# Attention and a snake MLP in one kernel: another order for the first two stages

## The chip, the cores and the metric

The kernel runs on one core of one Trainium2 chip. The metric is the device time of one execution in microseconds (us); it is the median of several runs. All times below are in microseconds unless marked otherwise. Five engines work side by side, each through its own queue in order: TensorE (PE, with its weight loads PEld), VectorE (DVE), ScalarE (ACT), GpSimd (POOL) and SyncE (SP). DMAs are issued by SP, ACT and POOL; all of them run on the same 16 DMA engines.

## The reference

Eight batches, twelve heads, 448 positions, head width 64. The queries and keys are normalised by their root mean square, attention follows, and its output (3584 tokens, 768 wide) goes through an MLP with a snake activation:

```python
q_n, k_n = rmsnorm(q, g_q), rmsnorm(k, g_k)
scores = q_n @ k_n.T / sqrt(64)
attn = softmax(scores)              # over the keys
x = (attn @ v), heads side by side  # 3584 x 768
h = x @ w_in                        # 768 x 2048
g = h + sin(alpha * h)**2 / (alpha + 1e-9)
out = g @ w_out                     # 2048 x 768
```

Inputs and output are f32; the matmuls run in bf16.

## The kernel before, in words

The work goes batch by batch, one stage per batch. A stage computes the attention of batch b, then h and g of batch b (`first_product`, L460), while the product with w_out of batch b-1 (`second_product`, L498) is cut into small filler steps that stand between the pieces of attention. Stage 0 has no fillers. After the last stage the last product runs by itself.

The twelve heads of a batch are three chunks of four (chunk index ci, three per batch, so ci 0 to 2 belong to batch 0). For each chunk: load q and k (`load_qk`, L155, on SP's queue, the k of chunk 0 on ACT's), square them (`square`, L274: on ACT for ci 0 and 1, on POOL after that), fold g_q times g_k into q (`fold_g`, POOL, L283), sum the squares (`reduce`, DVE, L288), take the inverse root (`rsqrt`, ACT, L292; for ci up to 3 the result lies in PSUM and holds a pair of banks), scale to bf16 (`scale`, L302: DVE for ci up to 3, POOL after that), and transpose, for ci 0 to 2 with PE (`pe_transpose`, L323, whose copies out of PSUM are on DVE or ACT), later with DMA transposes on SP's queue (L315). The tiles of q and k have three buffers, so chunk ci + 3 is loaded when chunk ci has been scaled.

Per batch there are 21 score tiles (3 chunks of 7): four matmuls into a pair of PSUM banks and one exp on ACT (`scores`, L348). Five running products use the exp tiles (`attend`, L385): sums and values of chunk 0 ("ones 0", "values 0") and of chunks 1 and 2 ("ones 1", "low 1", "high 1"). A finished sum becomes a reciprocal by Ln and Exp on ACT (L431, L432), a finished value product is multiplied by it on DVE into xT (L440). h then runs over xT with all of w_in: 16 blocks m, two per PSUM pair; Sin on ACT (L446), its square on POOL for even m and on ACT for odd m (L449, L451), the sum on DVE (L454).

PSUM is four pairs of banks. Which pair each user gets is written out by hand as a string of digits per stage, taken one by one (`bank_pair`, L134); a user waits until the last user of that pair is through.

The order is also written out by hand, as a string of tokens per stage (`STAGE_0`, `STAGE_1`, and `STAGE_N` for the rest), and each engine's queue holds its part of the tokens in that order. A token is a letter and its arguments: `q` square, `u` reduce, `g` fold_g, `r` rsqrt, `k` scale, `p` transpose with PE, `t` transpose with DMA, each with the chunk's number counted from the stage's first chunk, then which (0 is q, 1 is k) and, if need be, which heads; `l` loads q and k of a chunk. `S` is the next score tile, and `Sn` puts n dummy matmuls of 512 columns ahead of it; `bn` is n dummies alone. `o`, `v`, `x`, `y`, `z` go on with "ones 0", "values 0", "ones 1", "low 1", "high 1" by so many tiles j. `F` (or a number n, which is n times F) is the next filler step of the oldest unit, `f` one of the unit after it; a unit has 8 steps of 8 matmuls, and step s needs blocks 2s and 2s + 1 of w_out. `G` spreads the gains, `L` spreads alpha (one small matmul and a copy each). `W` and `O` load a piece of w_in (`W` half, third) and a quarter of w_out (`O` hi, lo: rows of blocks 8 hi + 4 lo and the next three), `V` a part of v of a later or the same batch (0, 1 or 2: one, three or two of the six head pairs), all on POOL's queue with a cast to bf16. `D` lets POOL wait for a chunk's k, so that what POOL issues behind it starts later. The third member of a stage lists tokens that stand beside h: key -1 early in it, key i after blocks 2i and 2i + 1, key 8 at its end.

## Time and profile before

| | |
|---|---|
| three runs | 407.88, 408.73, 409.87; median 408.73 |
| profiled execution: span of its instructions | 405.8 |
| profiled execution: its own time outside the span | not given |
| busy in the span | PE 391.4 (96%), DVE 240.6 (59%), ACT 315.3 (78%), POOL 283.6 (70%) |
| h of batch 0, first to last matmul group | 35.60 to 54.49 |
| h of batch 1 begins | 81.50 |

A row of a timeline gives the start, the duration of all its instructions together, the engine, the line, the operation with its tiles and shapes, the count, and in brackets how long the engine had been idle before and what ended that. A row of the chain gives start, duration and what held up the end. A busy PE is not PE at its peak, since the ends of matmuls are modelled.

### The profile page before, as it was taken

The page shows a single profiled execution, that of the slowest core. Times are in us where ns is not written, and L with a number is a line of the kernel's source. Part 1 is how long each engine was busy: PE and PEld are TensorE (multiplying, and loading weights), DVE is VectorE, ACT ScalarE, POOL GpSimd, SP SyncE. Part 2 cuts the span into 40 slices and gives each one's busy share as a digit, 9 for nine tenths or more (in the row PEclk, how much of TensorE's full clock was granted, in tenths as well). Part 3 has the DMA queues.
Part 4 walks back from the last instruction along what each step waited for, and adds up shares of the span by engine and source line. Part 5 has one row for each costly group of instructions (what it writes and reads, how often), then busy time and mean ns, then how long its engine had stood idle before and what let it go on. Part 6 is the DMA issues. An engine that isn't in the chain of part 4 may idle for free.

```text
span 405.8 us, 15218 instructions
## 1 busy us (share of the span) xinstructions
PE 391.4 (96%) x6755; PEld 238.8 (59%) x6758; DVE 240.6 (59%) x364; ACT 315.3 (78%) x474; POOL 283.6 (70%) x268
## 2 busy tenths in 40 slices
PE   1999999999999999999999999999999999999996
PEld 1346467645675566755676556755667556765564
DVE  4956665756783576638584475836685485544512
ACT  5798889868896879958898678958898679877600
POOL 5998889987959789588877779597895784003300
PEclk9999999999999999999999999999999999999999
DMA  7999999855286925697076923879046901620022
GB/s 266 215 254 241 210 221 255 193 155 171 53 164 162 151 94 88 182 198 153 3 140 178 200 102 70 185 158 209 3 94 179 166 2 22 108 61 1 2 78 79
DMA packets 67846, 55.46 MB, mean 137 GB/s; under 512 B 41524, under 2 KB 63172, under 8 KB 67780
## 3 DMA queue, kind: packets, MB, share of 16 engines
q1 hardware_dynamic: 56578, 41.43, 42.2%
q0 software_dynamic: 10432, 11.81, 19.0%
q8 instruction: 53, 0.87, 0.9%
q10 hardware_dynamic: 770, 1.25, 0.9%
q14 instruction: 13, 0.11, 0.1%
HBM read 45.62 MB, written 11.01 MB: 140 GB/s over the span
## 4 chain that ended last, share of the span: by engine, by line
PE 88%; POOL 5%; DMA 3%; issue 1%; DVE 1%; ACT 1%; SPq 0%; POOLq 0%
PE hps L468 34%; PE ops L548 31%; PE av L416 9%; PE sc L357 7%; PE ops L529 5%; POOL sq L281 2%; DMA qk<-in_q_dram 2%; DMA qk<-in_k_dram 2%; PE av L404 1%; POOL qk L286 1%; POOL w_out_sb L248 1%; POOL w_in L241 1%; ACT expT L360 1%; DVE g_sb L454 0%; DVE xT L440 0%
## 5 line engine op out<-in xcount | busy, mean ns | idle before, releaser
L360 ACT ACTIVATE expT<-sc 128x896 bf16<-128x896 f32 x168 | 143.7, 917 | 7.4 <-PE sc L357 6.6
L548 PE MATMUL ops<-w_out_sb,g_sb 64*64 64x384 bf16 x3072 | 148.0, 323 | 0.0
L468 PE MATMUL hps<-xT,w_in 128*128 128x448 bf16 x768 | 147.0, 353 | 0.4 <-DVE g_sb L454 0.4
L468 PEld LDWEIGHTS <-w_in 128*128 128x128 bf16 x768 | 74.4, 98 | 72.5 <-issue 3.9
L454 DVE SCALAR_TENSOR_TENSOR g_sb<-s,inv_alpha_sb,hps 128x448 bf16<-128x448 f32 x128 | 81.1, 676 | 59.1 <-POOL s L449 58.5
L548 PEld LDWEIGHTS <-g_sb 64*64 64x64 bf16 x3072 | 91.9, 107 | 37.0 <-issue 3.8
L449 POOL TENSOR_TENSOR s<-s 128x448 f32<-128x448 f32 x64 | 59.6, 932 | 65.7 <-ACT s L446 43.9
L446 ACT ACTIVATE s<-hps,alpha_sb 128x448 f32<-128x448 f32 x128 | 73.9, 627 | 37.7 <-PE hps L468 37.2
L309 POOL TENSOR_TENSOR qkn<-qk,inv 128x448 bf16<-128x448 f32 x80 | 72.9, 938 | 24.6 <-issue 17.1
L281 POOL TENSOR_TENSOR sq<-qk 128x896 f32<-128x896 f32 x44 | 73.3, 1678 | 3.9 <-DVE ms L290 3.0
L357 PE MATMUL sc<-qkT 64*64 64x448 bf16 x672 | 60.3, 357 | 0.7 <-ACT expT L360 0.3
L286 POOL TENSOR_TENSOR qk<-qk,gg 128x896 f32<-128x896 f32 (+1 forms) x25 | 50.5, 2021 | 2.2 <-ACT g_sb L278 1.5
L554 DVE COPY osb<-ops 128x384 f32<-128x384 f32 x48 | 26.7, 556 | 38.5 <-PE ops L548 38.3
L290 DVE TENSOR_REDUCE ms<-sq 128x14 f32<-128x896 f32 x44 | 46.4, 1078 | 3.3 <-POOL sq L281 3.2
L440 DVE TENSOR_TENSOR xT<-av,rec 128x896 bf16<-128x896 f32 (+1 forms) x26 | 25.7, 1016 | 26.8 <-ACT rec L432 21.4
L451 ACT ACTIVATE s<-s 128x448 f32<-128x448 f32 x64 | 36.9, 577 | 2.9 <-DVE g_sb L454 0.7
L416 PE MATMUL av<-expT,vb 64*32 64x448 bf16 (+1 forms) x1120 | 38.1, 350 | 0.0
L357 PEld LDWEIGHTS <-qkT 64*64 64x64 bf16 x672 | 21.7, 107 | 13.8 <-issue 6.7
L555 DVE TENSOR_TENSOR osb<-osb,ops 128x384 f32<-128x384 f32 x48 | 26.6, 554 | 1.7
L416 PEld LDWEIGHTS <-vb 64*32 64x32 bf16 (+1 forms) x1120 | 20.8, 96 | 11.0 <-issue 2.2
L429 DVE TENSOR_REDUCE rec<-rec 32x448 f32<-32x448 f32 x28 | 17.1, 610 | 9.7 <-ACT rec L425 9.4
L529 PE MATMUL ops<-w_out_sb,g_sb 128*128 128x384 bf16 (+1 forms) x144 | 21.0, 309 | 0.0
(51 smaller groups left out, 185.8 us busy)
## 6 DMA issues: line engine op xcount, KB each, us to landing
qk<-in_q_dram SPq DMA_DIRECT2D x23, 448.0 KB, 5.2
qk<-in_k_dram SPq DMA_DIRECT2D x23, 448.0 KB, 5.7
out_dram<-osb SPq DMA_DIRECT2D x45, 192.0 KB, 2.9
w_out_sb<-in_moe_w_out_dram POOLq DMA_DIRECT2D x4, 768.0 KB, 12.8
w_in<-in_moe_w_in_dram POOLq DMA_DIRECT2D x6, 512.0 KB, 12.2
vb<-in_v_dram POOLq DMA_DIRECT2D x16, 168.0 KB, 7.2
vb<-in_v_dram POOLq DMA_DIRECT2D x8, 224.0 KB, 5.3
out_dram<-osb SPq DMA_DIRECT2D x13, 96.0 KB, 4.3
```

What stands on the lines that cost most here:

```text
L281: nc.gpsimd.tensor_mul(st.sq[w], qk[ci][:, w], qk[ci][:, w])
L286: nc.gpsimd.tensor_mul(x, x, gg.to_broadcast([P, len(heads) * NJ, D]))
L290: nc.vector.reduce_sum(st.ms[:, w, rows], st.sq[w][:, rows], axis=AX.X)
L309: eng.tensor_mul(n[:, :, hi, :], x[:, hi], inv[:, hi].unsqueeze(2).to_broadcast([P, NJ, D]))
L357: nc.tensor.matmul(sc[o:o + 64, hi, :S], qkt[r, 1, j * REST:(j + 1) * REST], qkt[r, 0, :], start=True, stop=True)
L360: nc.scalar.activation(expT[c, j], sc[:, :, :S], ACT.Exp, scale=SCALE)
L416: nc.tensor.matmul(av[o, k, :S], w, x[r, hi, :], start=(j == 0), stop=(j == last))
L446: nc.scalar.activation(s1, hps, ACT.Sin, scale=alpha_sb[:, m, :])
L449: nc.gpsimd.tensor_mul(s2, s1, s1)
L454: nc.vector.scalar_tensor_tensor(g_sb[:, m, (b % 2) * S:(b % 2 + 1) * S], s2, inv_alpha_sb[:, m, :], hps, op0=ALU.mult, op1=ALU.add)
L468: nc.tensor.matmul(ps[:, m % 2, :S], w_in_sb[m * 2 // MT][:, kt, m % (MT // 2) * P:(m % (MT // 2) + 1) * P], x[:, kt, :], start=(kt == ORD ...
L548: nc.tensor.matmul(st["ps"][os, r, :HALF], g_sb[rs, m, c0 + o * 64:c0 + o * 64 + 64], w_out_sb[rs, m, half * HALF:(half + 1) * HALF], star ...
```

## The change

The tokens of the first two stages are put in another order, with other strings of PSUM pairs. Dummy matmuls (`b`) stand from the start of stage 0's queue, before L and G. V00, V01 and a quarter of w_out (O10) come early, the three tokens D are gone, W11, W10 and W12 move to the beginning of h (key -1), O01 and O11 into h, and the loads of v for batch 1 from the end of h to stage 1. The products o, v, x, y, z are cut into shorter runs. Some helpers change to allow this: a square and the copies after a transpose can name their engine (`A`, `P`, `D`), and the PSUM pair of an rsqrt is given back when its own scalings are done, not when all four of the chunk are.

```diff
 STAGE_0 = (
     (
-        "q000 u000 q010 G q011 q001 u010 g00 u011 r01 g01 D1 u001 k01 r00 k00 q11 u11 O00 q10 V00 p012 "
-        "W01 q20 p00 g1 u10 r1 q21 u20 V01 g2 S4 V02 S k11 l3 k10 S1 S1 S4 W00 W02 S u21 r2 p1 L S2 S q31 "
-        "S3 k21 q30 k20 D2 S S3 o3 l4 g3 S W10 W12 o1 o3 p2 u30 l5 S3 u31 S1 S W11 S4 v7 S S S q40 S S x5 "
-        "y3 q41 u41 x1 g4 z4 u40 x1 r4 y4 O01 q50 z3 r3 O10 "
+        "b2 V00 q010A b3 b4 b3 q000A b2 u000 u010 q001A L b1 G V01 q011A u011 b4 r01 O10 u001 k01 r00 b5 q10A "
+        "g01 q11A b1 g00 b1 p01A k00 p00A u10 g1 u11 r1 q20P b2 q21P g2 b1 S1 S3 k10 S2 k11 S u20 S2 p1D u21 "
+        "S S1 b1 W01 l3 r2 V02 S2 k20 k21 S S1 S3 p2D q31P S o2 o2 S o1 S l4 u31 W00 v1 q41 v2 q30P u41 O00 "
+        "o2 S5 S2 q40 u30 W02 S v1 v3 S y1 z1 S z2 z1 u40 S y4 S x2 x5 y1 y1 z3 g3 "
     ),
-    "012311203203312021021302301231032103021321302",
-    {-1: 'u50 O11 k30', 0: 'D4 k401', 1: 'k411', 2: 'q51', 3: 'k31 k400 u51', 5: 'k410', 7: 'g5 V12', 8: 't3 V10 V11 t4 l6 l7'},
+    "2321230132031232210031031203310210321301321302121213032103",
+    {-1: 'W11 r3 r4 l5 k31 k30 q50 g4 u50 W10 t3 W12 q51 g5', 0: 'k410', 2: 'k400 O01 l6', 4: 'u51 O11 k411', 6: 'k401', 7: 'q60 t4'},
 )
 STAGE_1 = (
     (
-        "4 r2 f f k20 1 f f 2 k21 S 1 q31 1 t2 S 1 S 2 S q30 2 S 2 S S 3 f S 3 S 1 f S 1 S 1 u31 2 l5 g3 "
-        "S u30 o1 o6 1 r3 V10 2 S f q41 1 f 2 S 2 S 2 q40 S u41 1 v1 v1 S v3 V12 S k31 q50 v2 u40 S 2 S "
-        "V11 g5 S z4 x7 y7 r4 z3 g4 k30 "
+        "1 f S r2 f f f 1 f q31 2 S u30 f 1 S 1 k20 1 l4 2 f 1 u31 S V00 V01 1 k21 S 3 S q40 1 S 2 S o2 o5 S "
+        "2 r3 S 4 f V02 1 q41 t2 1 S 2 g4 k31 S 3 S 1 S 2 u41 S 2 v1 S v2 S v2 v2 S 2 S 1 S y4 x1 y1 x3 S 2 "
+        "x3 z2 u40 y2 z2 z3 "
     ),
-    "1320201203203013133213130101301231203123",
-    {-1: 'u50 t3', 0: 'k41', 2: 'k40', 5: 'q51', 6: 'l6 t4', 8: 'u51 l7'},
+    "2103030201201302101301321213213310231023",
+    {-1: 'g3 V10 k30 V11 r4 k40 l5 t3 k41 q50 l6', 0: 'l7 t4 q51', 1: 'V12', 3: 'u51', 5: 'g5 u50'},
 )
...
-        def square(w, heads=(0, 1)):
+        def square(w, heads=(0, 1), engine=None):
             if ci < 2:
                 st.sq[w] = spare(2 * ci + w).rearrange("p (a d) -> p a d", d=D)
-                rows = slice(heads[0] * NJ, (heads[-1] + 1) * NJ)
-                nc.scalar.activation(st.sq[w][:, rows], qk[ci][:, w, rows], ACT.Square)
+            elif w not in st.sq:
+                st.sq[w] = npool.tile([P, 2 * NJ, D], F32, tag="sq", name="sq")
+            rows = slice(heads[0] * NJ, (heads[-1] + 1) * NJ)
+            x, out = qk[ci][:, w, rows], st.sq[w][:, rows]
+            if (engine or ("A" if ci < 2 else "P")) == "A":
+                nc.scalar.activation(out, x, ACT.Square)
             else:
-                st.sq[w] = npool.tile([P, 2 * NJ, D], F32, tag="sq", name="sq")
-                nc.gpsimd.tensor_mul(st.sq[w], qk[ci][:, w], qk[ci][:, w])
+                nc.gpsimd.tensor_mul(out, x, x)
...
             inv = bank_pair("inv") if early else ln
-            if early:
-                st.inv_ps.append(inv)
+            held = SimpleNamespace(ps=inv, left=2 * len(range(2)[ws]))
             for w in range(2)[ws]:
-                st.inv[w] = inv[:, w, :2 * NJ]
+                st.inv[w], st.inv_ps[w] = inv[:, w, :2 * NJ], held
...
-            st.scaled += len(heads)
-            if st.scaled == 4:
-                for ps in st.inv_ps:
-                    give_back(ps)
+            held = st.inv_ps[w]
+            held.left -= len(heads)
+            if early and held.left == 0:
+                give_back(held.ps)
...
-        def pe_transpose(pairs, ws=(0, 1), act=0):
+        def pe_transpose(pairs, ws=(0, 1), engines="D"):
...
-                if act == 1 or act == 2 and pp == 0:
+                engine = engines[pp % len(engines)]
...
+                if engine == "A":
                     nc.scalar.copy(out, src)
                 else:
                     nc.vector.tensor_copy(out, src)
```

## Rows read from the trace of the kernel before

**Rows 1.** The page: the chain that ended last, shares of the span by engine.
```profile
PE 88%; POOL 5%; DMA 3%; issue 1%; DVE 1%; ACT 1%; SPq 0%; POOLq 0%
```

**Rows 2.** The chain in order of time: start, duration, what.
```profile
40.69 0.94 POOL s L449
41.66 1.28 DVE g_sb L454 x2
...
54.49 3.70 PE ops L548 x88
...
81.50 1.62 PE hps L468 x8
...
99.96 2.40 PE ops L548 x56
...
128.61 18.27 PE hps L468 x96
```

**Rows 3.** Timeline of ACT in stage 0.
```profile
10.75 0.51 ACT L339 COPY qkT<-tp 128x448 bf16<-128x448 bf16 x1
13.43 0.32 ACT L299 ACTIVATE inv<-ms,eps 128x28 f32<-128x28 f32 x1 [2.17 <-DVE ms L290]
...
13.92 3.32 ACT L360 ACTIVATE expT<-sc 128x896 bf16<-128x896 f32 x4
...
26.32 7.46 ACT L360 ACTIVATE expT<-sc 128x896 bf16<-128x896 f32 x9
```

**Rows 4.** Timeline of PE in stage 0.
```profile
11.22 1.89 PE L352 MATMUL sc<-blank 128*128 128x512 bf16 x4
...
26.71 1.04 PE L352 MATMUL sc<-blank 128*128 128x512 bf16 x4
...
35.60 4.71 PE L468 MATMUL hps<-xT,w_in 128*128 128x448 bf16 x24
```

**Rows 5.** Timeline of DVE in stage 0.
```profile
0.87 0.27 DVE L201 MEMSET blank<- 128x256 uint32 x1 [0.87 <-PEq L665]
...
7.09 1.15 DVE L290 TENSOR_REDUCE ms<-g_sb 128x7 f32<-128x448 f32 x2 [0.63 <-ACT g_sb L278]
8.30 2.21 DVE L309 TENSOR_TENSOR qkn<-qk,inv 128x448 bf16<-128x448 f32 x4
10.43 1.08 DVE L290 TENSOR_REDUCE ms<-g_sb 128x14 f32<-128x896 f32 x1
```

**Rows 6.** Windows: length, busy by engine, granted PE clock, DMA share, GB/s.
```profile
10.00:20.00 10.00, 9.44 (x94) 3.59 (x90) 9.12 (x17) 7.50 (x14) 9.97 (x10) 1.00 1.01 214
```

**Rows 7.** Timeline of POOL in stage 0.
```profile
6.07 1.13 POOL L286 TENSOR_TENSOR qk<-qk,gg 128x448 f32<-128x448 f32 x1 [1.14 <-ACT g_sb L278]
...
14.95 1.67 POOL L281 TENSOR_TENSOR sq<-qk 128x896 f32<-128x896 f32 x1
...
17.89 2.10 POOL L286 TENSOR_TENSOR qk<-qk,gg 128x896 f32<-128x896 f32 x1
...
27.65 2.18 POOL L241 DMA_DIRECT2D w_in<-in_moe_w_in_dram  x3
```

**Rows 8.** DMA queues, 8.5 to 9.0 (q1 SP's): packets, MB, share.
```profile
q1 hardware_dynamic: 119, 0.20, 105.2%
```

**Rows 9.** DMA queues, 16.5 to 17.0 (q0 is POOL's; V loads).
```profile
q0 software_dynamic: 54, 0.05, 57.8%
q1 hardware_dynamic: 52, 0.09, 56.4%
```

**Rows 10.** DMA issues, 2.3 to 3: KB each, median us to landing.
```profile
qk<-in_k_dram SPq DMA_DIRECT2D x1, 448.0 KB, 6.5
```

**Rows 11.** DMA queues, 12 to 14: all that moved.
```profile
q0 software_dynamic: 253, 0.39, 110.2%
```

**Rows 12.** DMA issues, 9 to 9.9.
```profile
w_out_sb<-in_moe_w_out_dram POOLq DMA_DIRECT2D x1, 768.0 KB, 7.7
```

**Rows 13.** DMA issues, 38 to 39.
```profile
w_out_sb<-in_moe_w_out_dram POOLq DMA_DIRECT2D x2, 768.0 KB, 15.0
```

More of the change, by code (lines that the diff above doesn't have):

```diff
@@ L266, in norm_tasks @@
         st.ms = npool.tile([P, 2, 2 * NJ], F32, tag="ms", name="ms")
-        st.inv, st.inv_ps, st.scaled = {}, [], 0
+        st.inv, st.inv_ps = {}, {}
         st.sq, st.n = {}, None
@@ L578, in step @@
     def step(b, token):
-        what, n = token[0], [int(x) for x in token[1:]]
+        what, n = token[0], [int(x) for x in token[1:] if x.isdigit()]
+        engines = [x for x in token[1:] if not x.isdigit()]
         if what == "b":
@@ L610, in step @@
             elif what == "q":
-                st.square(n[1], n[2:] or (0, 1))
+                st.square(n[1], n[2:] or (0, 1), *engines)
             elif what == "u":
@@ L620, in step @@
             elif what == "p":
-                st.pe_transpose((0, 1), n[1:2] or (0, 1), act=n[2] if n[2:] else 0)
+                st.pe_transpose((0, 1), n[1:2] or (0, 1), engines or "D")
             elif what == "t":
```

## The prediction

> **What bounds the kernel now.** I read the chain of waits first. PE's own work makes up 88% of it [rows 1]. The chain in order of time [rows 2] says where the rest is: until 40.69 it runs through POOL, its DMA issues and the q and k loads; then DVE frees a PSUM pair, and from there to the end it is PE. So after the h product of batch 0 the time is a sum of matmuls that the change does not alter: stage 1 has 48 filler steps and 21 score tiles before and after. What the change can move is when that h product ends (54.49 [rows 2]) and how densely stage 1 is packed. Stage 1 takes 27.0 from there to its own h (81.50); the stage after it takes 28.65 (99.96 to 128.61) with 8 filler steps more, each 0.336 (88 matmuls, 11 steps, in 3.70). At that density stage 1 would take 25.95, so about 1.05 is the most to be had there.
>
> The start is read from the timeline of ACT [rows 3]. The first exp begins at 13.92, after the inv of pair chunk 1 waited 2.17 for DVE's sums. The 21st exp ends at 26.32 + 7.46 = 33.78. Between them ACT has 21 exps of 0.83, a reciprocal and an inv, and nearly no gap: 19.9 that end with ACT, whatever PE does. The h product begins at 35.60 [rows 4], 1.82 later. So stage 0 is: first exp, plus 19.9, plus a tail of 1.82, plus 18.89 for h (35.60 to 54.49), where stage 1's h takes 18.46 (81.50 to 99.96).
>
> **The change, part by part.** The sum is made against the profiled execution: its span is 405.8, its own time outside the span isn't shown, and the runs (407.88 to 409.87, median 408.73) are 2.1 to 4.1 longer. I take it as the median run, 2.9 around the span.
>
> *Dummies ahead of G.* Fourteen dummy matmuls, then L, one more dummy and G now stand at the head of PE's queue, where G alone had been. PE is free once blank is zero, at 1.14 [rows 5]. A dummy took 0.47 at 11.22, just after PE had been idle, and 0.26 at 26.71 [rows 4], for 512 columns each: the 1.2 GHz level of the clock and the 2.4 GHz level. So the fourteen end between 4.8 and 7.7. I take 6.8, near the low level, since PE comes from idling here too. L, a dummy, G and the copy of gg add about 1.3, an estimate from those prices: gg at 8.1, with bounds 6.1 and 9.0. The granted clock, on the other hand, is given as 1.00, the 2.4 GHz level, from 10 to 20 [rows 6], over those 0.47 dummies. The Trainium skill (TensorE: Matmul & The Clock Gate, Seeing it yourself) warns that the trace's clock events have been unreliable; by the granted clock as written the fourteen would end at 4.8, by the durations late, and I go by the durations.
>
> *From gg to the first exp.* DVE runs in order behind gg's copy: two reductions (1.15), four scalings (2.21), two reductions of 1.08 [rows 5]; then r1 on ACT, 0.49 from its start to the first exp [rows 3]. POOL's two folds of 1.13 [rows 7] lie beside the reductions and the first scalings. With 0.3 for handoffs that is 6.35: first exp at 14.5, against 13.92. The three copies out of PSUM that go from DVE to ACT (four of 0.51 there now [rows 3]) take about a microsecond off DVE, else it would be 15.5; they fit on ACT before r1 only if chunk 1's k has come.
>
> *V and w_out early, the D gates gone.* V00, V01 and the w_out quarter O10 are issued by about 7 on the POOL queue, without waiting for chunk 1. SP's queue alone moved 119 packets in half a microsecond [rows 8]; beside V loads it moved 52 to their 54 [rows 9]. The bounds for the early stretch: no loss (chunk 1's k landed 6.5 after its issue at 2.49 [rows 10], at 9.0), or SP shut out, as from 12 to 14, where 253 packets were all of the POOL queue's [rows 11]. I take sharing one for one, the row nearest in kind (V beside q and k). The Trainium skill (DMA: Bandwidth & Descriptors, Queues, rings and completion order) says the engines go round between queues packet by packet; by that rule sharing holds, and it speaks against issuing these loads early; rows 9 agree. The V bytes (0.45 MB at 0.05 in half a microsecond) keep the queues shared for 4.5: chunk 1's k lands about 1.0 late, at 10.05, and chunk 2's k, beside O10 too, some 4.4 late, at 15.7. At 10.05, ACT's square of 0.9 (near the exp of the same size), 4 copies of 0.51 and r1 end at 13.5: not the limit, but near.
>
> *POOL.* It stands until 15.7 for chunk 2's k (about 1.2 of idle time that before had not). From there it has, before the first s of h: 7 squares of 1.68, 4 folds of 2.10, 6 w_in issues of 0.73 and two more issues [rows 7], 26.0 in all: 41.7, where it was 40.69 [rows 2], as q51 and g5 now stand ahead of it and two w_out issues behind. All four PSUM pairs are free for h now (r3's pair is returned right after h begins, since k31 and k30 come up there), so PE needs the first pair back only 48 matmuls, 9.1, after h begins, and s 2.3 before that: by h + 6.8, or 43.2. It just fits. The late w_in halves are issued at about 37 and 38 into a queue that has run low; the early O10 is through long before. I cost them at nothing; the cover is 1 to 1.5, and what POOL loses beyond that falls on h one for one.
>
> *Shorter runs of o, v, x, y and z* are the same matmuls in other places. After the last exp there are 5 groups instead of 7, but x starts later, as its PSUM pair is that of the last tile but one: tail 1.75 for 1.82. The tile behind p2 waits for k20 and k21 to give a pair back: 0.3 of ACT's time. h then begins at 14.5 + 19.9 + 0.3 + 1.75 = 36.45, and with 18.4 for h (no 0.4 wait for a pair) ends at 54.85: 0.36 later than before.
>
> *Stage 1 and w_out's last quarters.* O01 is issued after five POOL passes of 0.94 [rows 2], at about 46.4, O11 at about 49.4. A quarter landed 7.7 after its issue into an empty queue [rows 12] and the last two a median of 15.0 after theirs, in a full one [rows 13]; this one is nearly empty: 54.1 and 57.1 (chunk 6 shares with them: up to a microsecond more). They are needed after 3 and after 12 filler steps, at 56.1 and 59.5. The first score tiles stand earlier, so ACT begins its exps some 0.3 sooner, but PE is the limit there. V of batch 1 and chunk 7's loads move into stage 1, some 8 before they are read. Bounds: 1.05 saved, up to 5 lost on w_out. I take 0.1 lost, being nearest to the empty queue.
>
> **Sum:** 0.36 + 0.1, about 0.5 later: span 406.3, time 409.2. About 0.5% (2.04) is what a measurement of this kernel can tell from no change, so I call this no change.
>
> **Rivals.** *The front is quicker.* If the clock is high at once, gg comes at 6.1, and the first exp is set by chunk 1's k: 13.5. h ends at 53.8 (0.7 earlier), and if stage 1 also gets the density of the later stages, 1.05 more: 407.0. For it speaks the granted clock of 1.00; against it the 0.47 dummies. Chance 0.24.
>
> *q and k are shut out* (slower). If SP's queue is held as from 12 to 14, chunk 1's k waits until V and O10, 1.24 MB as bf16 at 0.195 a microsecond, are through: from about 6.6 (an estimate of their first packet) to 12.9. Then ACT, in order, holds its copies behind q11: first exp at 12.9 + 0.9 + 2.04 + 0.49 = 16.3, 1.8 later than forecast, and all behind it: 411.0. It decides from a landing of chunk 1's k later than 11. For it: rows 11; against it: that was a transfer newly issued, these are under way already. The one-for-one rule of the skill speaks against it. Chance 0.2.
>
> *The change doesn't hide w_out.* If O01 lands 13 after its issue, as in a full queue, PE stands at the fifth m of unit 1 until 59.4, not 56.1: 412.5. Against it: little else is queued then. Chance 0.08.
>
> **How the numbers follow.** My case has 0.48, with a range of its own of 408.2 to 410.4 (the first exp between 13.5 and 15.4 by gg's bounds and chunk 1's landing). The range for all cases takes in the first two rivals and leaves out the third and the ends of w_out's bounds: 406.4 to 412.0. Faster by over 0.5% means below 406.7, just beyond the first rival: half of it, and 0.05 of mine with stage 1's gain on top, 0.17. Slower by over 0.5% means above 410.8: most of the second, the third, and a tail of mine, 0.26. Within: 0.57.
>
> **What would show it.** Right: the first dummies last 0.4 to 0.5; gg is copied near 8.1 and the first exp starts near 14.5, after DVE's sums; POOL idles until about 15.7 for chunk 2's k; the first s is at about 41.7; h of batch 0 ends near 54.9 with no wait for a PSUM pair; PE waits little for w_out. Wrong: ACT waiting for chunk 1's k beyond 11 (second rival), a first exp before 13.6 (first), PE waiting on w_out or w_in by over a microsecond, or a stage 1 much shorter than 27.

## The result, and the profile after

The change makes the kernel slower: a median of 413.23 us (412.45 to 416.71) against 407.81 for the kernel before, measured beside it; ratio 1.0144, interval 1.0115 to 1.0173. The profiled span grew from 405.8 to 411.6.

The page of the changed kernel, its chain by engine (compare [rows 1]), shows PE at 78 per cent for 88, and transfers at 6 for 3:

```profile
PE 78%; DMA 6%; POOL 6%; DVE 2%; ACT 2%; issue 2%; SPq 1%; POOLq 0%; ACTq 0%
```

Where it went is read from the timeline of PE: the beginnings of the h products (hps) and of the stages between them. First the kernel before, whose h of batch 0 begins at 35.60 [rows 4]:

```profile
54.42 3.77 PE L548 MATMUL ops<-w_out_sb,g_sb 64*64 64x384 bf16 x88
...
81.43 2.83 PE L468 MATMUL hps<-xT,w_in 128*128 128x448 bf16 x13
```

and the changed kernel:

```profile
35.50 2.50 PE L471 MATMUL hps<-xT,w_in 128*128 128x448 bf16 x12
38.78 7.55 PE L471 MATMUL hps<-xT,w_in 128*128 128x448 bf16 x39 [0.78 <-DMA w_in<-in_moe_w_in_dram]
48.36 8.69 PE L471 MATMUL hps<-xT,w_in 128*128 128x448 bf16 x45 [2.03 <-DMA w_in<-in_moe_w_in_dram]
56.98 0.84 PE L551 MATMUL ops<-w_out_sb,g_sb 64*64 64x384 bf16 x16
...
76.41 0.38 PE L360 MATMUL sc<-qkT 64*64 64x448 bf16 x2 [1.71 <-DMA qkT<-qkn]
...
86.62 18.33 PE L471 MATMUL hps<-xT,w_in 128*128 128x448 bf16 x96
```

So h of batch 0 begins 0.1 earlier and takes 21.48 for 18.82, with 2.81 of waiting for w_in; stage 1 up to its own h takes 29.64 for 27.01, with 1.71 of waiting for transposes of chunk 2. Those two are 5.3 of the 5.8. Of the rest, 0.44 is in stage 2 and wasn't followed up.

What was late in each is in the chain in order of time (start, duration, what). Both are transfers:

```profile
36.73 0.71 POOL w_in L241
37.44 10.88 DMA w_in<-in_moe_w_in_dram
...
67.54 1.33 SPq L321
...
68.97 7.40 DMA qkT<-qkn
```

The last piece of w_in, issued at 37.44, lands at 48.3, 12.8 after h began. In the kernel before it was issued at 29.11 and landed 14.5 later, at 43.6, only 8.0 after h began (w_in's last two pieces there, from issue to landing; the last figure is the last piece's):

```profile
DMA to landing us min/median/max: 12.7/13.6/14.5
```

What else those transfers had beside them is in the timeline of SP. Chunk 3's transposes t3, which SP issued at 49.65 before, and chunk 6's loads l6, at 56.8 before, now come while w_in is on its way:

```profile
40.75 3.85 SPq L321 DMA_TRANSPOSE qkT<-qkn  x2
44.72 0.52 SPq L164 DMA_DIRECT2D qk<-in_q_dram  x1
45.28 2.89 SPq L164 DMA_DIRECT2D qk<-in_k_dram  x1
```

Up to 44 both kernels had moved the same, 5.1 MB in POOL's queue and 5.05 in SP's. But behind the changed front two quarters of w_out stood ahead of w_in's last pieces, where there was one: of those 5.1 MB, V is 0.69 and two quarters are 1.57, so 0.32 of w_in's 3.15 was still to come, while the kernel before had all of w_in and 0.44 of the next quarter. Then, from 44 to 50 (queue: packets, MB, share; q0 is POOL's queue, q1 SP's), the changed kernel:

```profile
q1 hardware_dynamic: 1587, 0.40, 86.7%
q0 software_dynamic: 177, 0.33, 33.2%
```

and the kernel before:

```profile
q0 software_dynamic: 828, 1.23, 114.0%
```

The engines were as busy, but moved 0.73 MB instead of 1.23. The transposes' packets are small; and when w_in was through at 48.3, POOL's queue moved nothing until the first packet of O01 at 51.4, though O01 was issued at 46.68.

### The profile page after: what moved, and what is told of

It is laid out like the page before. It is cut to its first block, busy times and chain, and to the rows that moved or that the text cites. A ratio compares the mean times of both kernels' runs of the same rounds, so it can differ in the third digit from the quotient of the medians.

```text
span 411.6 us, 15271 instructions
## 1 busy us (share of the span) xinstructions
PE 399.3 (97%) x6781; PEld 243.0 (59%) x6784; DVE 240.1 (58%) x361; ACT 316.5 (77%) x477; POOL 283.8 (69%) x265
## 4 chain that ended last, share of the span: by engine, by line
PE 78%; DMA 6%; POOL 6%; DVE 2%; ACT 2%; issue 2%; SPq 1%; POOLq 0%; ACTq 0%
PE hps L471 29%; PE ops L551 27%; PE av L419 9%; PE sc L360 6%; PE ops L532 5%; DMA w_in<-in_moe_w_in_dram 3%; POOL sq L284 2%; DMA qkT<-qkn 2%; ACT expT L363 2%; DMA qk<-in_q_dram 1%; PE av L407 1%; POOL s L452 1%; DVE g_sb L457 1%; POOL qkn L311 1%; DVE ms L293 1%
## 5 line engine op out<-in xcount | busy, mean ns | idle before, releaser
L551 PEld LDWEIGHTS <-g_sb 64*64 64x64 bf16 x3072 | 94.7, 107 | 34.6 <-issue 3.8
L360 PE MATMUL sc<-qkT 64*64 64x448 bf16 x672 | 61.8, 353 | 2.1 <-DMA qkT<-qkn 1.7
L419 PE MATMUL av<-expT,vb 64*32 64x448 bf16 (+1 forms) x1120 | 39.7, 350 | 1.1 <-DVE xT L443 0.4
L360 PEld LDWEIGHTS <-qkT 64*64 64x64 bf16 x672 | 22.8, 106 | 15.2 <-issue 5.6
L432 DVE TENSOR_REDUCE rec<-rec 32x448 f32<-32x448 f32 x28 | 17.1, 610 | 10.8 <-ACT rec L428 10.6
```

The costliest lines, as they stand in the source:

```text
L360: nc.tensor.matmul(sc[o:o + 64, hi, :S], qkt[r, 1, j * REST:(j + 1) * REST], qkt[r, 0, :], start=True, stop=True)
L419: nc.tensor.matmul(av[o, k, :S], w, x[r, hi, :], start=(j == 0), stop=(j == last))
L551: nc.tensor.matmul(st["ps"][os, r, :HALF], g_sb[rs, m, c0 + o * 64:c0 + o * 64 + 64], w_out_sb[rs, m, half * HALF:(half + 1) * HALF], star ...
```

## Experiments

Theory A: h is late because w_in's last pieces are behind two quarters of w_out and then meet t3 and l6 on the DMA engines. Theory B: their issue from POOL is late. Theory C splits A: the second wait is t3's and l6's doing. Theory D: stage 1 is late because POOL issues t2 late. Later letters are explained in the expectations. All ratios are to the kernel before, measured beside each.

One reading needs care. Experiments 4 and 5 have the changed kernel's stage 0 word for word, and their waits for w_in are 1.48 and 1.28, and 1.17 and 1.83, where the changed kernel had 0.78 and 2.03. The sum repeats (2.76 to 3.00), a single wait doesn't. Steadier is when w_in's last piece lands: 10.8 to 11.1 after its issue in these three.

**1. O00 behind w_in.**
```diff
-q30P u41 O00
+q30P u41
-W10 t3 W12 q51 g5
+W10 t3 W12 O00 q51 g5
```


> The changed kernel, with the second early quarter of w_out (O00) issued behind the last piece of w_in instead of ahead of three of them. Theory A (the w_out quarters that now stand ahead of w_in fill the DMA engines, which are full from 31 to 45): a quarter took 3.9 of the POOL queue's time in the kernel before, so w_in lands about 3.9 earlier, both waits of h on w_in (0.78 and 2.03) go, h of batch 0 ends near 54.3 instead of 56.98, and the time falls by about 2.6, to 410.6. Theory B (the pieces of w_in are issued too late, behind POOL's squares and folds): their issue moves by 0.8 at most, so does the second wait, and the time falls by 0.8 or less. Theory C (the DMA transposes t3 take the engines while the last piece is under way): the piece would be through before them, and it can't be told from A by this run.

Measured: 1.0192 (1.0112 to 1.0272). PE's waits in its timeline:

```profile
34.94 9.88 PE L471 MATMUL hps<-xT,w_in 128*128 128x448 bf16 x51
45.74 8.69 PE L471 MATMUL hps<-xT,w_in 128*128 128x448 bf16 x45 [0.92 <-DMA w_in<-in_moe_w_in_dram]
57.39 0.38 PE L360 MATMUL sc<-qkT 64*64 64x448 bf16 x2 [1.76 <-DMA qkT<-qkn]
61.48 4.05 PE L551 MATMUL ops<-w_out_sb,g_sb 64*64 64x384 bf16 x48 [3.39 <-DMA w_out_sb<-in_moe_w_out_dram]
68.25 1.82 PE L551 MATMUL ops<-w_out_sb,g_sb 64*64 64x384 bf16 x40 [1.23 <-DMA w_out_sb<-in_moe_w_out_dram]
```

h falls to 19.42, near what A says, but only the first wait is gone; the second is still 0.92, where A expected none. Without the first, PE comes to w_in's last piece 9.9 after h's beginning (the 51 matmuls of the first row), and the piece lands 10.8 after it. The time comes back as 4.6 of waiting for w_out and 1.76 for transposes (stage 1 takes 37.3): what doesn't fit through the engines is only moved. The four runs lie far apart, from 413.38 to 422.04, so the ratio is rough.

**2. w_in issued earlier.**
```diff
-q40 u30 W02 S v1
+q40 u30 W02 W11 W10 W12 S v1
```
(and W11, W10, W12 gone from key -1.)


> The changed kernel, with W11, W10 and W12 issued right behind W02, some 2 to 5 earlier, ahead of the folds and squares of chunks 3 and 4; O00 stays where it is. Theory A (full DMA engines): the last piece lands at most 1 earlier, the second wait stays at 1 or more, and the time stays within 1 of 413.2. Theory B (issued too late): the wait of 2.03 goes, and the time falls by about 2.

Measured: 1.0106 (1.0074 to 1.0138). The waits for w_in are 1.40 and 0.97, h takes 21.04. Theory B falls: an earlier place in POOL's program gives 0.4.

**3. t3 and l6 later.**
```diff
-l5 k31 k30 q50 g4 u50 W10 t3 W12 q51 g5
+l5 q50 g4 u50 W10 W12 q51 g5
-2: 'k400 O01 l6'
+2: 'k400 O01', 3: 'k31 k30 t3 l6'
```


> The changed kernel, with the scalings of chunk 3 and its DMA transposes t3 (and the load of chunk 6 behind them) some 6 later in h, as they stood in the kernel before; the PSUM pair of chunk 3's inverse root is held that much longer, and h goes on with three pairs. Theory C (the transposes starve the last piece of w_in, which moves 0.02 to 0.05 MB a microsecond beside them and 0.2 without): that piece lands 1.5 to 2 earlier, the wait of 2.03 shrinks to 0.5 or less, h ends 1.2 to 2 earlier (0.4 may go to the held pair). Theory A alone: the wait stays within 0.5 of 2.03.

Measured: 1.0274 (1.0242 to 1.0306). The wait for w_in is 0.91, the second one is gone, as C says, but C is only part of it. Without t3 and l6 beside it w_in's last piece lands 9.4 after its issue, where the changed kernel had 10.9 (the last two pieces):

```profile
DMA to landing us min/median/max: 7.6/8.5/9.4
```

That is 1.4 of the 2.03; the rest is hidden, since PE had stood 0.52 for a PSUM pair before it came there. The total says nothing on C: my numbering of the PSUM pairs gave the last tile of h the pair that stage 1 takes first, and PE stood 3.10 for it at 60.11.

**4. V behind k21.**
```diff
-V00 V01 1 k21 S
+1 k21 V00 V01 S
```


> The changed kernel, with the loads V00 and V01 of batch 1 issued behind the scaling k21 of chunk 5 instead of between k20 and k21. Theory D (these loads hold up k21, and their data the transposes t2, which hold up the first score tile of chunk 2): the transposes are issued 1.9 earlier, PE's wait of 1.7 on them goes, stage 1 (29.6 from the first filler to the first matmul of h) falls to 27.5 to 28, and the time falls by 1.6 to 2.2, to about 411.3. Rival (stage 1 is longer for other reasons, the transposes being late because h ended 2.5 late): less than 0.6 is saved.

Measured: 1.0123 (1.0092 to 1.0154); stage 1 takes 29.65, no gain. t2 was issued 9.13 into the stage instead of 10.56, but chunk 2's first score tile still waits, in two parts:

```profile
76.58 0.38 PE L360 MATMUL sc<-qkT 64*64 64x448 bf16 x2 [1.38 <-DMA qkT<-qkn]
77.30 0.38 PE L360 MATMUL sc<-qkT 64*64 64x448 bf16 x2 [0.35 <-DMA qkT<-qkn]
```

With V's loads now right behind t2, the transposes, issued from 66.84, are slower by what they were issued earlier. Theory D falls.

**5. t2 first.**
```diff
-f q31 2 S u30 f 1 S 1 k20 1 l4 2 f 1 u31 S V00 V01 1 k21 S
+k20 f k21 t2 q31 2 S u30 f 1 S 2 l4 2 f 1 u31 S V00 V01 1 S
```
(and t2 gone from its old place behind q41.)


> The changed kernel with one part of the second stage in another order: the scaling of chunk 2 of batch 1 and its transposes (k20 k21 t2) stand ahead of the squares q31 and of V00, V01 on POOL, so that t2 can be issued about 62.5 instead of 67.5. Theory E (stage 1 is long because t2 is issued late and then takes 7 to 10 on busy DMA engines, against a first use 2 earlier than in the kernel before): PE's wait of 1.7 for qkT at about 76 is gone and stage 1 takes 27.3 to 28.2 instead of 29.6; the total falls by 1.4 to 2.3, to about 411 to 412. Rival F (the DMA engines are the limit, so the transposes issued sooner only push back others): a wait of 1 to 3 for another chunk's transposes or for the V loads takes its place, stage 1 stays at 29 to 30, and the total at 413.

Measured: 1.0196 (1.0143 to 1.0249). The wait for qkT is gone and stage 1 takes 28.90, 0.7 less, but PE now waits for an output buffer:

```profile
69.79 0.84 PE L551 MATMUL ops<-w_out_sb,g_sb 64*64 64x384 bf16 x16 [1.27 <-DVE osb L558]
```

The timeline of SP says why: t4's and t2's transposes held its queue for 10.5, and the first output stores stood behind them.

```profile
58.11 10.52 SPq L321 DMA_TRANSPOSE qkT<-qkn  x4
...
69.90 1.20 SPq L519 DMA_DIRECT2D out_dram<-osb  x2
```

h of batch 1 took 20.1 instead of 18.5, so the total is no better than the changed kernel's (1.0196 for 1.0144, and the intervals overlap).

**6 and 7. Both cures, and one quarter less ahead of w_in.** Experiment 5's order, with t3 and l6 at the end of h and q60 in stage 1 as q30:
```diff
-l5 k31 k30 q50 g4 u50 W10 t3 W12 q51 g5
+l5 k30 q50 g4 u50 W10 W12 q51 g5
-2: 'k400 O01 l6'
+2: 'k400 O01', 3: 'k31'
-7: 'q60 t4'
+8: 't3 t4 l6'
```
then, in 7, O10 from behind r01 to behind W12.


> As the run before it, and in h of batch 0 the transposes t3 and the loads l6 go to the end, as in the kernel before (k31 at key 3, so that t3 can't be issued before about 48; t3, t4, l6 at key 8; the squares q60 move into stage 1 behind t2). Theory A+E (w_in's last part is held up by t3's transposes and l6's loads on the DMA engines, and stage 1 by t2): the second wait of PE for w_in (2.0) is gone, the first (0.8) stays because two quarters of w_out still stand ahead of w_in: h of batch 0 takes 19.2 to 20.0, stage 1 27.3 to 28.2, total 408.5 to 410. Rival G (the bytes of both queues together are what runs out, so that h or stage 1 pays at another place): h plus stage 1 stay at 50 to 51, with waits for w_out or for chunk 3 of batch 1, and the total at 412 or more.

> As the run before it, and the quarter O10 of w_out moves from the first microseconds to right behind w_in's last piece, so that only one quarter of w_out stands ahead of w_in, as in the kernel before. Theory A+E: PE waits for w_in less than 0.2 in all, h of batch 0 takes 18.6 to 19.0, stage 1 27.3 to 28.2, and the total is that of the kernel before within 0.4 per cent (407 to 409.5). Rival G: O10, O01 and O11, some 2.4 MB, don't land before stage 1 reads them, and PE waits 1 to 4 for w_out at about 58 to 62; the total stays over 411.

Measured: 1.0234 (1.0191 to 1.0276) and 1.0395 (1.0322 to 1.0467). In 6 the only wait for w_in is 0.43, in 7 there is none, but in both PE waits 2.9 and 3.8 for PSUM pairs within h (again my numbering) and 2.5 for qkT at the beginning of stage 1. In 7 h also begins 3.8 late, at 39.34: without O10 POOL waited until 27.1 for chunk 4's k (22.3 in the changed kernel), its sums held VectorE, PE stood 1.96, and its clock then fell (window: length, busy by engine, PE's granted clock, DMA share):

```profile
34.00:38.00 4.00, 4.00 (x88) 1.46 (x96) 0.03 (x1) 2.10 (x3) 3.98 (x3) 0.57 1.16 200
```

Neither settles the sum. On w_in 6 agrees with 3: its last piece lands 9.5 after its issue, and PE, which had stood 1.01 for a pair, finds it there. In 7 h began so late that the missing wait shows little.

**8. The new front, the old h's end and the old stage 1**, with PSUM pairs renumbered to fit.
```diff
-l5 k31 k30 q50 g4 u50 W10 t3 W12 q51 g5
+l5 k30 q50 g4 u50 W10 W12 q51
-2: 'k400 O01 l6'
+2: 'k400 O01', 3: 'k31'
-7: 'q60 t4'
+7: 'g5 V12', 8: 't3 V10 V11 t4 l6 l7'
```


> The changed kernel's plan of the first stage up to h of batch 0, with the h of the kernel before (t3's second scaling k31 at key 3, V12, V10, V11, t3, t4, l6, l7 at the end) and its second stage; the PSUM pairs are renumbered so that the hand-over to the second stage is the one of the kernel before. Theory A (what costs in h is that t3 and l6 run beside the last of w_in and w_out; what the new front has put ahead of w_in costs under 1): h of batch 0 begins at 35.3 to 36.0, takes 18.8 to 19.8 with one wait for w_in of 0.4 to 1.2, stage 1 takes 27.0 to 27.4, and the total is 407.5 to 409.5, ratio 1.000 to 1.005. Rival H (the new front itself costs it, since O10 and O00 ahead of w_in leave w_in or w_out short): h over 20.5 or PE waits for w_out in stage 1, total over 410.5.

Measured: 1.0136 (1.0076 to 1.0195). One wait for w_in of 1.33, h 20.44, stage 1 33.0. The queues from 46 to 50 show something new:

```profile
q0 software_dynamic: 44, 0.07, 23.8%
```

In these 4 us only the end of w_in (landed at 47.8) and, from 49.3, the beginning of O01 moved, with nothing beside them. O01 was issued at 47.76, from behind POOL's scalings and products, so POOL's queue stood nearly empty. PE then waited 0.26 for w_out at 60.17, and in stage 1 stood 1.51 and 2.15 for what the profile puts down to nothing. So the late issue of O01 and O11 may be a cost of its own (Theory J); in the changed kernel t3 and l6 run in that hole. The total, 413.53, is what Rival H said (over 410.5), though the profile is of the slowest of the four runs (416.68; the others took 411.99 to 413.67). That PE waits for w_in only once here proves little on t3: the last piece lands 9.8 after its issue, 11.8 after h's beginning, and PE comes as late, having lost 1.33 for w_in and 0.39 for a pair.

**9, 10 and 11. O01 and O11 issued early**: in the changed kernel (9), in experiment 8's kernel (10), and there with O00 behind w_in too (11).
```diff
-W12 q51
+W12 O01 q51
-0: 'k410'
+0: 'k410 O11'
```


> The changed kernel with w_out's last quarters issued earlier: O01 right behind w_in's last piece W12 (key -1) and O11 at key 0, instead of at keys 2 and 4 of h of batch 0. The run before (the new front with the old h's end) showed the POOL queue empty from 46 to 50, since w_in had landed and O01 was issued only at 47.76. Theory J (the late issue of O01 and O11 from within h leaves the queue dry, and the 0.8 MB that don't move there are paid for later): here t3's transposes still take the engines from 45 to 50, but w_out's last bytes land by about 58 instead of 61 and l4, t4 and t2 are less held up: h of batch 0 21.0 to 21.6 as in the changed kernel, stage 1 27.8 to 28.8 instead of 29.6, total 411.3 to 412.8. Theory A alone (only the transposes in the way of w_in count): all within 0.5 of the changed kernel, stage 1 at 29.4 to 29.9, total 412.8 to 414.

> The run with the new front and the old h's end and second stage, with O01 right behind W12 and O11 at key 0 as in the run before this one. Theory J: the POOL queue moves 0.4 MB in every 2 us from 42 to 53, PE's wait for w_out and the stalls of stage 1 are gone; h of batch 0 begins at 35.3 to 36.1 and takes 19.4 to 20.2 (one wait of 0.8 to 1.4 for w_in), stage 1 takes 27.0 to 27.8, total 408 to 410, ratio 1.001 to 1.006. Theory H (the new front has put the loads behind for good, wherever O01 and O11 are issued): stage 1 over 29, total over 411.

> As the run before it, and the quarter O00 moves from ahead of W02 to behind W12, so that only O10 stands ahead of w_in. Theory J: PE's wait for w_in falls to under 0.5, h of batch 0 takes 18.6 to 19.2, w_out still lands before it is read, stage 1 27.0 to 27.8, and the total is that of the kernel before within 0.4 per cent (406.5 to 409.3). Theory H: w_out is late instead, with PE waits of 1 to 4 for it in stage 1, total over 411.

Measured: 9 1.0232 (1.0189 to 1.0275), 10 1.0119 (1.0080 to 1.0158), 11 1.0152 (1.0110 to 1.0195). In 10 the queue ran full from 46 (1.11 MB from 44 to 50, 6.93 MB by 54, where the kernel before had 6.98), but with O01 beside it w_in's last piece again landed only at 48.7, 11.1 after its issue:

```profile
48.76 8.69 PE L471 MATMUL hps<-xT,w_in 128*128 128x448 bf16 x45 [1.24 <-DMA w_in<-in_moe_w_in_dram]
```

So the second wait isn't special to transposes, and C was too narrow: whatever moves beside w_in's last pieces makes them late. In 9 O01 was beside them as well as t3, the waits for w_in grew to 0.94 and 2.65, and t3's issue held SP for 10.1. In 11 PE didn't wait for w_in, having stood 1.38 for a PSUM pair before, and w_out was late (1.02 at 60.40), as in experiment 1. My expectation of about 408 to 410 for 10 and 11 was wrong: stage 1 took 29.1 in 10, with a stall of 1.66 at 76.97 that the profile puts down to nothing, and 33.7 in 11. So was that of 411.3 to 412.8 for 9, which took 417.38. Theory J's gain came in none of the three (10 took 413.01, 8 had taken 413.53), and Theory H's numbers came: stage 1 over 29 and the total over 411 in 10, a wait for w_out and the total over 411 in 11. So the new front lost time in 8, 10 and 11, wherever O01 and O11 were issued.

**12, 13 and 14. Parts alone, in the kernel before**: t3 and l6 in h (12), O01 and O11 in h (13), O10 early (14).
```diff
-{-1: 'u50 O11 k30',
+{-1: 'u50 O11 k30 k31 t3',
```
(12; l6 at key 2.)
```diff
-r4 y4 O01 q50 z3 r3 O10
+r4 y4 O10 q50 z3 r3
```
(13; O01 at key 2, O11 at key 4.)
```diff
-O00 q10 V00 p012
+O00 q10 V00 O10 p012
```
(14; O10 gone from the end of the plan.)


> The kernel before with one part of the change alone: chunk 3's second scaling k31 and its transposes t3 right after k30 in h of batch 0 (key -1), and l6 at key 2, instead of at the end of h. w_in's last piece is issued where it was, so PE should not wait for it. Theory T (transposes and loads of SP's queue beside the POOL queue take its engines): the POOL queue moves under 0.6 MB in 44 to 50 instead of 1.23, O11 lands 4 to 6 later and t4, t2 with it; h of batch 0 stays at 18.4 to 19.2, PE waits 0.5 to 3 for w_out or qkT in stage 1, total 409 to 411.5. Rival O (only the order of what stands ahead of w_in costs): h and stage 1 as before, total 407 to 408.6.

> The kernel before with the part that names the change alone: w_out's quarters O01 and O11 issued in h of batch 0 (keys 2 and 4), O10 in O01's old place. Theory J (issued from behind the scalings and the products of h, they leave the POOL queue dry): the queue is empty for 1 to 4 between 42 and 50, the last quarter lands at about 57 to 60 instead of 53, t3 and t4, which are issued at 49 to 57, run beside it, and PE waits 0.3 to 2.5 in stage 1; total 408.6 to 411. Rival: w_out's last quarters aren't read before 60, so it costs nothing, total 407 to 408.5.

> The kernel before with one quarter of w_out more ahead of w_in: O10 right behind O00 and the first piece of V, as the changed kernel has two quarters ahead of w_in's last pieces. Theory H (a quarter more ahead of w_in makes its last pieces late, by the 0.39 MB that it moves, some 2 at the queue's 0.42 MB per 2): PE waits 1 to 3 for w_in in h of batch 0, stage 1 stays at 27.0 to 27.5, total 408.8 to 411. Rival: w_in still lands in time, since before's queue has all of it by 44 and its last piece isn't read before 46: h 18.4 to 19.0, total 407 to 408.5.

Measured: 12 1.0037 (1.0005 to 1.0069), 13 1.0121 (1.0078 to 1.0164), 14 1.0105 (1.0065 to 1.0145).

In 12 h takes 18.81 with no wait for w_in, which was through by then: t3 and l6 do nothing to h when w_in isn't late. POOL's queue moves 0.88 MB from 44 to 50 (I expected under 0.6); PE waits 1.03 for qkT at 64.42, and stage 1 takes 29.4. From 46 to 48 the two queues move the same number of packets:

```profile
q0 software_dynamic: 215, 0.33, 93.0%
q1 hardware_dynamic: 215, 0.06, 23.1%
```

In 13 the queue is nearly dry from 46 to 50, as Theory J says, though w_in was in time:

```profile
q0 software_dynamic: 88, 0.12, 36.5%
```

The last quarter lands at 58.8, t3 and t4 beside it hold SP for 9.4, the stores come late behind t2, and PE stands for an output buffer, after which 40 matmuls take twice their time, at a clock of 0.57 from 74 to 78:

```profile
74.11 3.17 PE L548 MATMUL ops<-w_out_sb,g_sb 64*64 64x384 bf16 x40 [2.01 <-DVE osb L555]
```

That is the largest of the three: moving O01 and O11 into h loses 4.6 by itself (412.83 for 408.27). PE didn't wait for w_out here; most of the loss stands in this row, the wait for the buffer and the slow matmuls behind it. In 14 h takes 18.82 without a wait for w_in, so PE doesn't feel Theory H's price; but the price is there. w_in's last piece, issued at 29.49 (29.11 before), lands at 46.7 instead of 43.6 (the last two pieces):

```profile
DMA to landing us min/median/max: 15.4/16.3/17.3
```

One quarter more ahead of it costs it 3.1. PE doesn't feel it because h begins as much late, at 38.75, as V's last piece came late for stage 0:

```profile
30.81 1.51 PE L416 MATMUL av<-expT,vb 64*64 64x448 bf16 x26 [1.30 <-DMA vb<-in_v_dram]
```

So whether a quarter more ahead of w_in would be paid in h of this kernel stays open.

**15. The new stage 1 behind the old stage 0**, tried in two ways, since the new stage wants chunk 6 before the old stage 0 loads it; the squares q30, q31 were put behind k21, and their sums u30, u31 behind q30 and q31 in the first way, behind o5 in the second.
```diff
-7: 'g5 V12', 8: 't3 V10 V11 t4 l6 l7'
+7: 'g5', 8: 't3 t4 l6'
-1 k21 S 3 S q40
+1 k21 q30 q31 S 3 u30 S u31 q40
```


> The kernel before with the changed kernel's second stage alone (batch 1's V loads, l4 and the early scores inside it); since l6 comes at the end of h here, its squares q30 and q31 stand behind k21, so that t2 can be issued some 3 earlier than in the changed kernel. Theory E (the second stage's order is as good as the old one once chunk 2's transposes come in time): h of batch 0 18.4 to 18.9, stage 1 27.0 to 28.0, total 407.5 to 409.5. Rival I (the order itself costs, because the V loads now share the DMA engines with the transposes t2 and with l4 and the stores, wherever t2 is issued): stage 1 28.5 to 30, with waits for qkT or osb, total 409.5 to 411.5.

> The kernel before with the changed kernel's second stage, as in the run of that name before, but with the squares q30, q31 and their sums so late that VectorE isn't held up (there PE had stood 3.89 for an output copy). Theory E (the new order of stage 1 is as good as the old one when chunk 2's transposes come in time): h of batch 0 18.4 to 19.0, stage 1 27.0 to 28.0, total 407.5 to 409.5. Rival I (V's loads and l4 beside the transposes and the stores make it longer in any case): stage 1 28.5 to 30, total 409.5 to 411.5.

Measured: 1.0145 (1.0085 to 1.0205) and 1.0182 (1.0143 to 1.0220). Both are inconclusive: PE stood 3.89 for an output copy behind sums of chunk 6 in the first, 3.57 for an exp in the second, and its clock fell to 0.60 and 0.50 after that.

**16 and 17. The new stage 1 word for word, with l6 early** (experiment 12's stage 0, q60 at key 7), and the same with V's loads at the end of h.
```diff
-7: 'q60 g5', 8: 't4'
+7: 'q60 g5', 8: 'V10 V11 V12 t4'
-V00 V01 1 k21
+1 k21
```
(17 against 16; V02 gone too.)


> The first stage of the kernel before with t3 and l6 early in h (the run in which that stood alone, whose h took 18.8 without a wait for w_in), and behind it the second stage of the changed kernel word for word, with q60 at the end of h. Theory E (its second stage loses by chunk 2's transposes, issued behind q31, V00 and V01 on POOL and then 7 to 10 on the way beside V's loads): h of batch 0 18.6 to 19.2, one wait of 1 to 3 for qkT at about 72 to 74, stage 1 29.0 to 30.2, total 408.8 to 411. Rival K (stage 1 of the changed kernel is long only because w_out's last 1.1 MB still move when it begins): with w_out landed by 55 stage 1 takes 27.0 to 28.2, total 406.8 to 408.6.

> As the run before it, with V's loads for batch 1 (V10, V11, V12) issued at the end of h of batch 0, as in the kernel before, in place of V00, V01 and V02 within stage 1. Theory E: V is through before t2 is issued, the transposes land 4 to 6 after issue instead of 7 to 10, PE's wait for qkT is under 0.5 and stage 1 takes 27.2 to 28.4; total 407 to 409. Rival (V's place doesn't matter): within 0.6 of the run before it.

Measured: 1.0165 (1.0131 to 1.0199) and 1.0110 (1.0078 to 1.0142). In 16 h takes 18.82 and stage 1 32.47, with two waits for transposes:

```profile
57.77 0.38 PE L357 MATMUL sc<-qkT 64*64 64x448 bf16 x2 [2.99 <-DMA qkT<-qkn]
76.47 0.38 PE L357 MATMUL sc<-qkT 64*64 64x448 bf16 x2 [1.89 <-DMA qkT<-qkn]
```

The first is for t3, which POOL's full queue had slowed (chain):

```profile
41.93 15.79 DMA qkT<-qkn
```

The old stage 1 takes eleven filler steps (88 matmuls) before its first score tile, the new one two, so the old one didn't feel this in 12. Without the first wait 29.5 is left, what the changed kernel takes. Rival K isn't tested by this: it needed w_out landed by 55, and the last quarter landed at 57.1, 3.6 after stage 1 began, where the changed kernel has 4.1. In 17 the second wait is gone: the second of t2's transposes lands at most 4.3 after its issue (72.16), without V's loads beside it, where it took 5.4 in 16. But PE also comes there later, since a wait of 1.30 for an output buffer (osb, at 69.46) stands before it, as in experiment 5, and stage 1 takes 31.93. Theory E is right that V's loads slow t2, and wrong on the gain: 0.5 in the profiled stage 1 instead of 2, though the medians lie 2.2 apart (414.47 and 412.27). That the new order of stage 1 itself costs is my reading, not shown: Rival K stays open, and how the 0.9 beyond the wait for t2 comes about wasn't separated.

No version here beats the kernel before, or suggests one: each part that was tried alone loses time (12 only just). Nor does the new front bring h forward: in the eleven profiles that have it (7, without O10, left out) h of batch 0 begins between 34.94 and 36.34, in the seven with the old one (14, with O10 early, left out) between 34.50 and 35.93, so the 0.1 of the first pair of profiles lies within their spread.

## Why the prediction was wrong

I forecast 409.2 (406.4 to 412.0) and no change; it is 413.2, slower.

*The front: right in its working, and no gain.* The fourteen dummies end at 6.43 (I took 6.8), 0.37 each, under the 0.4 to 0.5 that I named, and gg is copied at 7.47 (8.1; timelines of PE and DVE):

```profile
1.20 5.23 PE L255 MATMUL ps<-blank 128*128 128x512 bf16 x14 [1.20 <-DVE blank L201]
```

```profile
7.47 0.23 DVE L225 COPY gg<-gps 128x64 f32<-128x64 f32 x1 [0.22 <-PE gps L224]
```

From there to the first exp, at 13.76, is 6.29 (6.35). Sharing one for one was too dark: from 6 to 10 SP's queue moved 711 packets to 215 of POOL's, and chunk 2's k, issued at 4.86, landed at 13.1, not 15.7, so POOL didn't stand for it as I had it. The tail behind the last exp was 1.3, not 1.75. h began at 35.50 where I had 36.45.

*POOL before h: right in its sum, by luck in its time.* The first s is at 41.85 (41.7), and no pair of h was waited for. But POOL came to q21, chunk 2's k, at about 13.9 and not at 15.7, and lost 2.2 later, waiting for the k of chunks 3 and 4 and for DVE's sums, which I hadn't costed. The two errors cancel. O01 is issued at 46.68 (46.4), O11 at 51.92 (49.4):

```profile
41.85 0.94 POOL L452 TENSOR_TENSOR s<-s 128x448 f32<-128x448 f32 x1
...
46.68 0.81 POOL L248 DMA_DIRECT2D w_out_sb<-in_moe_w_out_dram  x1
```

*The step that failed first* is "The late w_in halves are issued at about 37 and 38 into a queue that has run low; the early O10 is through long before. I cost them at nothing". They were issued at 36.7 and 37.4 into a full queue (its share was 107 per cent from 36 to 44): O10 was through but had taken the time in which w_in would have moved, and O00 stood ahead too. I counted when each piece is issued, not how many bytes stand ahead of it. The term that I had at nothing measured 2.81. I had looked at t3 and l6 only as instructions of SP, and at what l6 might do to O01 ("up to a microsecond more"), not at what they do to w_in. The bytes ahead are the larger part. PE, unhindered, comes to w_in's last piece 9.9 after h's beginning. The piece lands 8.0 after it in the kernel before and 12.8 in the changed one; 10.8 with O00 out of the way (experiment 1); 11.4 to 11.8 with t3 and l6 out of the way (3, 6, 8), still too late for PE. So t3 and l6 cost it 1.0 to 1.4, and the rest lies in what stands ahead; 14 shows that price by itself, 3.1 for one quarter. 2 shows that an earlier issue hardly helps (0.4), 12 that the transposes do nothing when w_in is through, 10 that O01 beside it does as much as they (the piece lands 13.0 after h's beginning).

*The second* is stage 1: "I take 0.1 lost, being nearest to the empty queue". POOL's queue was nearly empty, as I had it, but the engines weren't: t3 and l6 had them, and O01 landed at about 57, 3 later than I had it, O11 at about 61, 4 later. PE didn't wait for w_out, only since h was late itself. What PE waited for was chunk 2's transposes, which I hadn't costed at all: I only counted that V and chunk 7 come "some 8 before they are read", not what V's loads do to the transposes beside them. Stage 1 came out 2.63 longer, of which 1.71 is that wait; 17 against 16 shows that V's loads slow t2 by about 1 (5.4 from issue to landing, at most 4.3 without them). The cause of the other 0.9 stays open, and so does Rival K.

*The time outside the span* I took as 2.9, the median run less the profiled span. In every profiled run here it is 1.7 to 1.9 (413.33 for 411.6 in the changed kernel). With that my sum would have given about 408.1. The error of 1.1 lay on the side of the result: by luck the forecast looks nearer than its working was, a span 0.5 longer where 5.8 came.

*The rivals.* None of the three had the mechanism. The third, "The change doesn't hide w_out", is the nearest in its number, 412.5, but not in its mechanism: O01 did land late, 10.5 after its issue, yet PE came to it later still, and it was w_in that paid. Experiment 1 shows the wait that this rival describes, in another setting: there O01 landed 15.5 after its issue and PE stood 3.39 for it.

*What I said would show it wrong* did: PE waited for w_in by over a microsecond.

## What to carry to other kernels

Where the DMA engines were full here, a transfer's landing was set by the bytes ahead of it and the packets beside it, not by its issue: before moving a load, add up for each queue what has moved by the time of each first use. A transfer that is moved forward is paid for by the next one behind it, and transposes by DMA, whose packets are small, pay most. And a load issued from the middle of an engine's in-order work can leave its queue dry, though the engines are the bound before and after (experiments 8 and 13).

## What the runs showed of the hardware

- Transposes on SP's queue and loads on POOL's move the same number of packets where both have work (215 and 215 in 2 us in experiment 12), while a packet of the one carries about 0.3 KB and of the other 1.5 KB. So t3's two transposes, which land 5.7 and 6.3 us after their issue in the kernel before, where POOL's queue ran dry 3.5 to 5 after they were issued, took 13.8 and 15.8 in experiment 16, beside a POOL queue that was full until 57. The Trainium skill (DMA: Bandwidth & Descriptors, Queues, rings and completion order) says that the engines go round the queues by packets; experiment 12 agrees, and the cost of it lies with the queue of small packets. The changed kernel's 46 to 48 doesn't show one for one (441 packets to 43): there POOL's queue had little left, by my reading.
- A stall can cost twice: after PE stood for 1.96 (experiment 7), 2.01 (13) and 2.65 (9) its granted clock was 0.57 of full in the 4 us from 34, 74 and 49, which is the level of 1.2 GHz (0.50) for most of them; in 9 the 45 matmuls behind the stall took 10.37 instead of 8.69. The stall of 2.03 for w_in in the changed kernel left it at 1.00. What sets the two apart isn't shown.
- The first exp came between 13.20 and 14.60 in the eleven profiles that have the changed front, so that a difference of a microsecond there, in one profile, is no finding.
